# A smaller descriptor ring, five values buffers, tiles at one remainder of 512 bytes, four buffers of activated values, and a copy taken ahead on ScalarE

## The chip, the cores and the metric

The kernel runs on one core of a Trainium2 chip. The metric is the device time of one execution in microseconds. Before the change it is 827.01 us, the median of three runs (826.94 to 827.95).

## What is computed

```
def reference(**kwargs):
    ...
    attn_out = _attn_ref(**attn_kwargs)          # windows of 32 queries, 64 keys each, softmax, times v
    B, H, S, D = attn_out.shape                  # 2, 8, 768, 64
    x = np.ascontiguousarray(attn_out.transpose(0, 2, 1, 3)).reshape(B * S, H * D)
    x = _moe_ref(x=x, **moe_kwargs)              # sum over 4 experts e: p_e * (relu(x @ w1[e]) @ w2[e]), F = 1024
    return _moe2_ref(x=x, **moe2_kwargs)         # h = x @ w_in; (max(h,0) + alpha*min(h,0)) @ w_out, F = 2048
```

1536 tokens of width 512 go through a windowed attention, then through a layer of four weighted experts, then through a second layer with a leaky activation.

## The kernel before

Tokens are the moving side. The two feed-forward layers are cut into 24 slices `p` of the hidden width (16 of the experts, `NP1`, and 8 of the second layer) and each slice into two tiles of 384 columns. One tile is a `gemm1` (seven products of six matmuls, 42 in all, that make four hidden blocks by a scheme with sums of blocks) and a `gemm2` (48 matmuls into `y`, which VectorE adds to `acc`). Every number is split into a high and a low part, `wh`/`wl` for weights, `xh`/`xl` for tokens, `gh`/`gl` in `gg` for hidden values. ScalarE rounds the high part, and GpSimd (at times VectorE) takes the difference. The order of a tile on TensorE is `a b d a c d c`, then `y`.

Attention fills the first 70 us. It is done in twelve units of two halves. SyncE loads queries and keys (`qk`, ring of four halves, `load_half`) and values (`v`, `load_v`); TensorE makes scores (`two`), transposes (`t`), products with the values (`x`) and transposes back (`xt`); five idle matmuls (`keep`) fill each unit's wait. From the ninth unit on, the first expert's tile is mixed in.

Nothing is scheduled by hand in a table: `product` adds an estimated time to `now` for each matmul and, before each, polls streams of other work that are due by then (`prep_poll` for weights and transition, `lag_poll` for the activation steps put off with `later`). What comes out is a fixed program order on each engine, and each engine works it off in order. All transfers are issued from SyncE, one after the other, each on the eighth earlier one's semaphore.

Names that matter below:

- `v_t`: before, halves 0, 1 and 2 of each four stand in buffers of tags `w2`, `w2` and `fr`, the fourth in `w2`; from half 16 (`V_HOME`) in a tile `v4` of tag `S`, set to zero by VectorE when it is made. A values tile is 4160 bytes a partition, so a `w2` or `fr` buffer is 4160 bytes too, though the weights in it take 4096.
- `gelu`: in the second layer ScalarE takes `relu(-h)` out of PSUM (`ACTIVATE g<-a`), multiplies by `-alpha` (`ACTIVATE g<-g,nalpha`), VectorE adds `max(h, 0)`, ScalarE rounds into `gg` and GpSimd takes the rest. `g` has two buffers.
- `act.copy(u2, q["a"])`: the copy of a tile's first product. The second product on bank `a` writes the same bank, so TensorE waits for this copy.
- `prep_w1` for the second slice does not start before the last attention unit has passed its third stage (`att["stage"][NU - 1] > 3`), because it needs the `S` buffer that `v4` holds.

Where the tiles stand in the built program, as the byte address in a partition less the next lower multiple of 512: `xh` and `xl` 0, the ring of first weights 384, the four `w2` buffers 0, 64, 128 and 192, `fr` 256, `ft` 320, `raw` 320 and 384, `gg` of even tiles 0 and of odd tiles 384. In the slices 15 and 17 (`WIDE`) three of the seven first weights stand in `ft` and `fr` buffers instead of the ring (`w` in the rows, not `wh`/`wl`). After the change every one of these is 0.

Of the kernel before, what the change touches and what calls it, by code (L numbers as in the profile page):

```python
# [10 lines left out]
F32 = mybir.dt.float32  # L11
# [3 lines left out]
AF = mybir.ActivationFunctionType  # L15
# [3 lines left out]
B, H, S, D = 2, 8, 768, 64  # L19
# [3 lines left out]
NW = BLK // WIN  # L23
# [5 lines left out]
NU = B * NBLK  # L29
NT, DM = B * S, H * D  # L30
E, F1, F2 = 4, 1024, 2048
P = 128
KD = DM // P
HH = H // 2
HP = HH // 2
QW, KW = HP * BLK, HP * SPAN
NCOL = NT // 2
NP1 = E * F1 // (2 * P)
# [27 lines left out]
def tile_kernel(ctx: ExitStack, tc: tile.TileContext, qk, v, wa, wq, dpt, alpha, out):  # L66
    nc = tc.nc
    scale = 1.0 / float(D) ** 0.5
    pe_, dve, act, pool, sync = (Pinned(tc, e) for e in (nc.tensor, nc.vector, nc.scalar, nc.gpsimd, nc.sync))
# [3 lines left out]
    bp = ctx.enter_context(tc.tile_pool(name="bp", bufs=1))  # L73
# [29 lines left out]
    now = [0.0]  # L103
# [88 lines left out]
    def mm(*a, n, took=None, **kw):  # L192
# [2 lines left out]


    qk_t = [bp.tile([P, QW + KW], F32, tag="ggB", bufs=4, name=f"qk{i}") for i in range(RING)]
    v_t = [bp.tile([P, 2, HP, NW, D + 1], F32, name=f"v{i}", **tag) for i, tag in (
        (3, dict(tag="w2", bufs=4)), (0, dict(tag="w2", bufs=4)), (1, dict(tag="w2", bufs=4)), (2, dict(tag="fr")))]
    v_t = v_t[1:] + v_t[:1]  # L200
    for vt in v_t:
        for e in range(2):
            (pool, dve)[e].memset(vt[:, e], 0.0)
# [3 lines left out]
    pe = pe.rearrange("p (z k e) -> p z k e", e=2, k=KEYS)  # L207

    def v_of(hu):
        return v_t[hu % 4 if hu < V_HOME or hu % 4 < 3 else 4]  # L210

    def load_half(hu):
        if hu >= 2 * NU:
# [5 lines left out]
    def load_v(hu):  # L219
        assert hu == v_next[0]  # L220
        v_next[0] += 1
        if hu >= 2 * NU:
            return
        if hu == V_HOME:
            v_t.append(bp.tile([P, 2, HP, NW, D + 1], F32, tag="S", name="v4"))
            dve.memset(v_t[4], 0.0)
        for e in range(2):
            sync.dma_start(v_of(hu)[e::2, e].rearrange("p z w d -> p (z w d)"), v[hu // 2, e, :, hu % 2])

    def unit(u):  # L230
# [36 lines left out]
        for z in range(2 * HP):  # L267
            half, i = divmod(z, HP)
            if z in CUT:
                n = CUT[z]  # L270
                parts.append((z, n, bank(f"x{u}_{z}")[:, :2 * n * (D + 1)].rearrange("p (z e d) -> p z e d", e=2, d=D + 1)))
            z0, _, x_ps = parts[-1]
            for w in range(NW):
                mm(x_ps[win[w], z - z0], pt[:, z, win[w]], v_of(2 * u + half)[:, :, i, w], n=2 * (D + 1), took=T_X,
                   start=True, stop=True)
            if i == HP - 1:
                load_v(2 * u + half + 4)
        dn = cp.tile([P, 2 * HP, 2, 1], F32, tag="dn", bufs=2, name=f"dn{u}")
        for z, n, x_ps in parts:
            dve.tensor_scalar_add(dn[:, z:z + n], x_ps[:, :, :, D:D + 1], 1e-9)  # L280
# [176 lines left out]
    def pause(t, cond=None):  # L457
        return now[0] + t, cond

    def prep_w1(p):  # L460

        e, dt = pace(p in QUICK, p)
        combine = e
        if p == 1:
            combine = dve
        elif p == NP1:
            combine, dt = dve, DT_NEAR
        if p == NP1 + 2:
            yield pause(0.0, lambda: (NP1, 0) in used1)
        yield pause(0.0, lambda: (p, 0) in raws and (p == 0 or began and landed[p, 0] <= now[0] and att["stage"][NU - 1] > 3))  # L470
        raw = raws[p, 0]
        a11, a12, a22, a21 = (raw[:, i] for i in range(4))
        s = bp.tile([P, 4, 256], F32, tag="S", name=f"s_{p}")
        src = {A11: a11, A12: a12, A22: a22, S1: s[:, 0], S2: s[:, 1], S3: s[:, 2], S4: s[:, 3]}
        for zo, x, y, op in (
            (S1, a21, a22, ALU.add), (S2, s[:, 0], a11, ALU.subtract),
            (S3, a11, a21, ALU.subtract), (S4, a12, s[:, 1], ALU.subtract),
        ):
            combine.tensor_tensor(out=src[zo], in0=x, in1=y, op=op)
            if p:  # L480
                yield pause(dt)
        if p == 0:
            yield pause(4.5)
        for j, z in enumerate(USE):
            yield pause(0.0, lambda: room_w1(p, j))
            h, l = place_w1(p, j)
            act.copy(h, src[z])
            if p:
                yield pause(dt)
            e.tensor_tensor(out=l, in0=src[z], in1=h.bitcast(F32), op=ALU.subtract)  # L490
            w1[p, z] = (h, l)
            yield pause(dt)
        raws.pop((p, 0))
        if p == NP1 + 1:
            load_raw(p, 1)
        elif 0 < p < NP - 1:
            yield pause(0.0, lambda: conv_done(p + 1))
            load_raw(p + 1, 0)
# [131 lines left out]

    glist = []
    lag = []

    def later(t, f):
        lag.append((now[0] + t, f))
        lag.sort(key=lambda x: x[0])

    def lag_poll(until=None):
        while lag and (lag[0][0] <= now[0] or until is not None and not until()):
            lag.pop(0)[1]()  # L640

    def product(*a, n, **kw):
# [6 lines left out]
    def gemm1(p, c0, n, parity, last):  # L649
        cs = slice(c0, c0 + n)  # L650
        nm = f"{p}_{c0}"
        q = {}

        def prod(z, a, b, start, stop):
            if start:
                q[z] = bank(f"{z}{nm}")[:, :n]
            prep_force("w", lambda: (p, a) in w1)
            while p == 0 and b >= T4 and att["x"] < -(-(c0 + n) // BLK):
                att_poll(force=True)
            wh, wl = w1[p, a]  # L660
            k = 0
            for kd in range(2):
                f = slice(kd * P, (kd + 1) * P)
                for w_, x_ in ((wh, xh), (wh, xl), (wl, xh)):
                    product(q[z], w_[:, f], x_[:, 2 * b + kd, cs], n=n,
                            start=start and k == 0, stop=stop and k == 5, skip_group_check=True)
                    k += 1
            if last:
                used1.add((p, USE.index(a)))

        def add(z, other, out):
            dve.tensor_tensor(out=out, in0=q[z], in1=other, op=ALU.add)

        def tmp(name):
            return bp.tile([P, 384], F32, tag=name, name=f"{name}{nm}")[:, :n]

        gs = {}

        def gelu(blk, src):

            i, ab = divmod(blk, 2)

            lag_poll(lambda: len(glist) < 2 or glist[-2][1] in glist[-2][0])
            glist.append((gs, blk))
            if p >= NP1 and i == 0:
                if ab == 0:
                    g2 = bp.tile([P, 2, 384], F32, tag="pb", bufs=2, name=f"g2_{nm}")
                    gs["g2"] = g2
                g = gs["g2"][:, ab, :n]
            else:  # L690
                g = bp.tile([P, 384], F32, tag="g", bufs=2, name=f"g{blk}_{nm}")[:, :n]
            gg = bp.tile([P, 2, 384], F32R, tag="gg" + "AB"[parity], bufs=4, name=f"gg{blk}_{nm}")
            gh, gl = gg[:, 0, :n], gg[:, 1, :n]

            def high():
                act.copy(gh, g)
                pool.tensor_tensor(out=gl, in0=g, in1=gh.bitcast(F32), op=ALU.subtract)
                gs[blk] = (gh, gl)

            def whole():  # L700
                dve.scalar_tensor_tensor(out=g, in0=src, scalar=0.0, in1=g,
                                         op0=ALU.max, op1=ALU.add)
                later(0.8, high)

            if p < NP1:
                pb = pb_t[2 * p * P // F1, c0, n]
                dve.scalar_tensor_tensor(out=g, in0=src, scalar=0.0, in1=pb[:, ab, :n],
                                         op0=ALU.max, op1=ALU.mult)
                later(0.7, high)
            else:  # L710
                fi = 2 * (p - NP1) + i

                act.activation(g, src, AF.Relu, scale=-1.0)
                act.mul(g, g, nalpha[:, fi:fi + 1])
                later(1.4, whole)

        prod("a", A11, B11, True, False)
        u2 = tmp("u2")
        act.copy(u2, q["a"])
        prod("b", S2, T2, True, True)  # L720
        add("b", u2, u2)
        prod("d", S1, T1, True, False)
        t = tmp("t")
        add("d", u2, t)
        prod("a", A12, B21, False, True)
        gelu(0, q["a"])
        prod("c", S3, T3, True, False)
        add("c", t, q["b"])
        prod("d", S4, B22, False, True)
        gelu(3, q["b"])  # L730
        add("d", u2, q["d"])
        prod("c", A22, T4, False, True)
        gelu(1, q["d"])
        add("c", u2, q["c"])
        gelu(2, q["c"])
        return gs
# [120 lines left out]

    for hu in range(RING):
        load_half(hu)
    for hu in range(4):  # L860
        load_v(hu)
    stream("w", weights())
    streams["w"][0] = PREP0
# [79 lines left out]
X_WAIT = (0.0, 7.5)  # L943
DT_NEAR = 0.8
RING = 4
V_HOME = 16
WARM = 18
PAD = 16

# [73 lines left out]
```

## Time and profile before

| | |
|---|---|
| median of three runs | 827.01 us |
| the profiled execution | 827.0 us, span 825.2 us |
| TensorE busy | 812.6 us (98%), 5637 matmuls |
| VectorE, GpSimd, ScalarE busy | 578.7 (70%), 563.5 (68%), 330.8 us (40%) |
| transfers | 71.69 MB, 87 GB/s over the span, but 250 to 280 GB/s in the first 60 us |

A row of the profile is one instruction or a merged run of them. A matmul of 384 columns is listed with 0.34 us, but the next one starts some 0.175 us later, so what a stretch costs TensorE is read from starts, not from durations.

### The profile page before, as it was taken

To read this page: it belongs to the slowest core of one execution; us is meant where nothing else is said; L and a number is where in the kernel's file an instruction comes from. 1 tells how busy PE (TensorE), PEld (TensorE's weight loads), DVE (VectorE), ACT (ScalarE), POOL (GpSimd) and SP (SyncE) were. 2 spreads that over 40 slices of the span, in tenths; PEclk is the share of its full clock that TensorE was granted. 3 is DMA by queue.
4 is the path that set the end of the run, shared out by engine and by line. 5 is a ranking of instruction groups with operands and counts; after the bars stand their busy time and mean duration, and the time that the engine had idled before them with its cause. 6 is when DMAs were issued, how large, how long until landed. Compare 5 with 4: busy or idle time off the path is not lost.

```text
span 825.2 us, 14876 instructions
## 1 busy us (share of the span) xinstructions
PE 812.6 (98%) x5637; PEld 797.0 (97%) x5637; DVE 578.7 (70%) x1116; ACT 330.8 (40%) x718; POOL 563.5 (68%) x586
## 2 busy tenths in 40 slices
PE   8899999999999999999999999999999999999998
PEld 6678999999999999999999999999999999999998
DVE  4687477777777768767777677578954877756555
ACT  3666433223224123232332223145572665455441
POOL 2767777777877877967877872193954987866611
PEclk9999999999999999999999999999999999999999
DMA  7882121331331431322432312001002142211004
GB/s 251 248 279 81 51 90 52 122 115 46 115 103 39 134 116 45 115 71 74 126 102 81 112 37 69 10 26 52 27 26 90 46 122 81 73 40 52 0 1 153
DMA packets 30503, 71.69 MB, mean 87 GB/s; under 512 B 4704, under 2 KB 9952, under 8 KB 30432
## 3 DMA queue, kind: packets, MB, share of 16 engines
q1 hardware_dynamic: 30432, 70.75, 26.5%
q8 instruction: 44, 0.72, 0.4%
q14 instruction: 27, 0.22, 0.1%
HBM read 59.18 MB, written 11.56 MB: 86 GB/s over the span
## 4 chain that ended last, share of the span: by engine, by line
PE 90%; DMA 2%; POOL 2%; ACT 2%; DVE 2%; issue 1%; SPq 1%; ACTq 0%; DVEq 0%; POOLq 0%
PE y L60 47%; PE a L60 12%; PE c L60 11%; PE d L60 11%; PE b L60 6%; POOL gg L60 1%; DMA raw<-in_wa 1%; PE two L60 1%; ACT g L60 1%; DMA qk<-in_qk 1%; PE x L60 1%; DMA v<-in_v 1%; PE t L60 1%; SPq L60 0%; PE wps0.0_84 L60 0%
## 5 line engine op out<-in xcount | busy, mean ns | idle before, releaser
L60 PE MATMUL y<-gg,wh 128*128 128x384 f32 x1540 | 401.1, 337 | 0.7 <-POOL gg L60 0.5
L60 POOL TENSOR_TENSOR gg<-g,gg 128x384 fp32r<-128x384 f32 x192 | 200.9, 1056 | 122.4 <-ACT gg L60 107.8
L60 PEld LDWEIGHTS y<-gg,wh 128*128 128x128 f32 x1540 | 278.8, 188 | 1.8 <-POOL gg L60 1.2
L60 PE MATMUL y<-gg,wl 128*128 128x384 f32 (+1 forms) x770 | 258.6, 336 | 0.0
L60 DVE TENSOR_TENSOR acc<-y,acc 128x384 f32<-128x384 f32 x321 | 171.0, 550 | 53.5 <-PE y L60 52.1
L60 ACT CAST gg<-g 128x384 fp32r<-128x384 f32 x192 | 97.6, 512 | 169.3 <-DVE g L60 169.1
L60 POOL TENSOR_TENSOR wl<-raw,wh 128x256 fp32r<-128x256 f32 (+1 forms) x112 | 114.8, 1034 | 51.4 <-ACT wh L60 37.2
L60 PEld LDWEIGHTS y<-gg,wl 128*128 128x128 f32 x770 | 144.5, 188 | 0.0
L60 ACT COPY u<-a 128x384 f32<-128x384 f32 x48 | 23.0, 479 | 185.4 <-PE a L60 185.4
L60 POOL TENSOR_TENSOR wl<-s,wh 128x256 fp32r<-128x256 f32 x88 | 68.4, 784 | 8.7 <-ACT wh L60 8.1
L60 DVE TENSOR_TENSOR u<-b,u 128x384 f32<-128x384 f32 x48 | 26.7, 557 | 60.6 <-PE b L60 58.1
L60 PE MATMUL a<-xh,wh 128*128 128x384 f32 x184 | 62.4, 339 | 0.4 <-ACT u L60 0.4
L60 PE MATMUL d<-xh,wl 128*128 128x384 f32 x184 | 62.3, 338 | 0.0
L60 PE MATMUL d<-xl,wh 128*128 128x384 f32 x184 | 62.2, 338 | 0.0
L60 PE MATMUL d<-xh,wh 128*128 128x384 f32 x184 | 62.2, 338 | 0.0
L60 PE MATMUL a<-xl,wh 128*128 128x384 f32 x184 | 62.1, 338 | 0.0
L60 PE MATMUL a<-xh,wl 128*128 128x384 f32 x184 | 62.1, 338 | 0.0
L60 ACT CAST wh<-raw 128x256 fp32r<-128x256 f32 (+1 forms) x116 | 54.5, 491 | 15.6 <-PE y L60 14.2
L60 PE MATMUL c<-xh,wh 128*128 128x384 f32 x176 | 59.9, 340 | 0.2 <-DVE b L60 0.2
L60 PE MATMUL c<-xl,wh 128*128 128x384 f32 x176 | 59.5, 338 | 0.0
L60 PE MATMUL c<-xh,wl 128*128 128x384 f32 x176 | 59.5, 338 | 0.0
L60 POOL TENSOR_TENSOR fl<-fl,fm 128x512 f32<-128x512 f32 x32 | 41.4, 1294 | 26.5 <-DVE fm L60 17.5
(117 smaller groups left out, 1363.7 us busy)
## 6 DMA issues: line engine op xcount, KB each, us to landing
fr<-in_wq SPq DMA_DIRECT2D x32, 512.0 KB, 3.9
raw<-in_wa SPq DMA_DIRECT2D x28, 512.0 KB, 3.9
w2s<-fl SPq DMA_DIRECT2D x32, 256.0 KB, 2.4
raw<-w2s SPq DMA_DIRECT2D x16, 512.0 KB, 3.6
qk<-in_qk SPq DMA_DIRECT2D x24, 312.0 KB, 4.6
v<-in_v SPq DMA_DIRECT2D x48, 130.0 KB, 4.1
outT<-acc SPq DMA_DIRECT2D x15, 192.0 KB, 1.8
pb<-p_dram SPq DMA_DIRECT2D x6, 384.0 KB, 3.4
```

The costliest lines, as they stand in the source:

```text
L60: return self.tc.keep_in_program_order(f(*a, **kw))
```

## The change

- The ring that is kept at address 0 of each partition for descriptors of transfers issued by GpSimd is 2048 bytes instead of 16384. No transfer here is issued by GpSimd. 14 KB a partition come free.
- Values get five buffers all through (`RING_V`), two of them of a tag of their own; `v4`, its zeroing in the middle of the attention and `V_HOME` go. `load_v` runs five halves ahead.
- A values tile takes 1152 numbers, 4608 bytes, nine times 512 (`V_ROOM`), so the buffers that it shares with `w2` and `fr` begin at multiples of 512.
- `prep_w1` of the second slice no longer waits for the last unit's third stage.
- `g` has four buffers.
- In the second layer the negative part goes through `later`, and `hold` keeps put-off steps back until a tile's `u2` copy is issued, if nothing forces them.

```diff
+VW = 2 * HP * NW * (D + 1)
...
-    v_t = [bp.tile([P, 2, HP, NW, D + 1], F32, name=f"v{i}", **tag) for i, tag in (
-        (3, dict(tag="w2", bufs=4)), (0, dict(tag="w2", bufs=4)), (1, dict(tag="w2", bufs=4)), (2, dict(tag="fr")))]
-    v_t = v_t[1:] + v_t[:1]
+    v_t = [bp.tile([P, V_ROOM], F32, name=f"v{i}", **tag)[:, :VW].rearrange("p (e z w d) -> p e z w d", e=2, z=HP, w=NW)
+           for i, tag in enumerate((dict(tag="w2", bufs=4), dict(tag="w2", bufs=4), dict(tag="fr"), *2 * [dict(tag="v", bufs=2)]))]
...
-        return v_t[hu % 4 if hu < V_HOME or hu % 4 < 3 else 4]
+        return v_t[hu % RING_V]
...
-        if hu == V_HOME:
-            v_t.append(bp.tile([P, 2, HP, NW, D + 1], F32, tag="S", name="v4"))
-            dve.memset(v_t[4], 0.0)
...
-                load_v(2 * u + half + 4)
+                load_v(2 * u + half + RING_V)
...
-        yield pause(0.0, lambda: (p, 0) in raws and (p == 0 or began and landed[p, 0] <= now[0] and att["stage"][NU - 1] > 3))
+        yield pause(0.0, lambda: (p, 0) in raws and (p == 0 or began and landed[p, 0] <= now[0]))
...
+    hold = [False]
...
-        while lag and (lag[0][0] <= now[0] or until is not None and not until()):
+        while lag and (not hold[0] and lag[0][0] <= now[0] or until is not None and not until()):
...
-                g = bp.tile([P, 384], F32, tag="g", bufs=2, name=f"g{blk}_{nm}")[:, :n]
+                g = bp.tile([P, 384], F32, tag="g", bufs=4, name=f"g{blk}_{nm}")[:, :n]
...
-                act.activation(g, src, AF.Relu, scale=-1.0)
-                act.mul(g, g, nalpha[:, fi:fi + 1])
-                later(1.4, whole)
+                def negative():
+                    act.activation(g, src, AF.Relu, scale=-1.0)
+                    act.mul(g, g, nalpha[:, fi:fi + 1])
+                    later(1.4, whole)
+
+                later(0.0, negative)
+
+        hold[0] = p >= NP1
         prod("a", A11, B11, True, False)
         u2 = tmp("u2")
         act.copy(u2, q["a"])
+        hold[0] = False
...
-    for hu in range(4):
+    for hu in range(RING_V):
         load_v(hu)
...
-V_HOME = 16
+V_ROOM = 1152
+RING_V = 5
...
-    nc = _bacc.Bacc("TRN2", target_bir_lowering=False, num_devices=1)
+    nc = _bacc.Bacc("TRN2", target_bir_lowering=False, num_devices=1, dynamic_dma_scratch_size=2048)
```

TensorE's order does not change anywhere. On SyncE, at the start of the program, these are the issues of before (a `qk` row is one half's queries and keys, two `v` transfers are one half's values, `raw` are weights):

```order
L60 DMA qk3_112<-in_qk 128x624
L60 DMA v0_114<-in_v 64x520 x2
L60 DMA v1_115<-in_v 64x520 x2
L60 DMA v2_116<-in_v 64x520 x2
L60 DMA v3_113<-in_v 64x520 x2
L60 DMA qk0_109<-in_qk 128x624
L60 DMA qk1_110<-in_qk 128x624
L60 DMA raw0_0_179<-in_wa 128x256 x2
```

And now, at the same place:

```order
L61 DMA qk3_112<-in_qk 128x624
L61 DMA v0_113<-in_v 64x520 x2
L61 DMA v1_114<-in_v 64x520 x2
L61 DMA v2_115<-in_v 64x520 x2
L61 DMA v3_116<-in_v 64x520 x2
L61 DMA v4_117<-in_v 64x520 x2
L61 DMA qk0_109<-in_qk 128x624
L61 DMA qk1_110<-in_qk 128x624
L61 DMA raw0_0_184<-in_wa 128x256 x2
```

The fifth half's two transfers stand ahead of the third unit's `qk`, and all later `qk` and `raw` transfers of the attention stand two places further back.

On ScalarE, at the border of the two tiles of slice 18 in the second layer (`a18_384` is the next tile's first product, `c18_0` this tile's last), before:

```order
L60 ACTIVATE g2_18_0_7470<-g2_18_0_7470,nalpha_83 128x384
L60 CAST gg3_18_0_7495<-g3_18_0_7494 128x384
L60 ACTIVATE g2_18_0_7520<-c18_0_7474 128x384
L60 ACTIVATE g2_18_0_7520<-g2_18_0_7520,nalpha_83 128x384
L60 COPY u218_384_7533<-a18_384_7524 128x384
L60 CAST gg1_18_0_7513<-g2_18_0_7470 128x384
```

And now:

```order
L61 ACTIVATE g2_18_0_7471<-g2_18_0_7471,nalpha_83 128x384
L61 CAST gg3_18_0_7496<-g3_18_0_7495 128x384
L61 COPY u218_384_7532<-a18_384_7523 128x384
L61 ACTIVATE g2_18_0_7521<-c18_0_7473 128x384
L61 ACTIVATE g2_18_0_7521<-g2_18_0_7521,nalpha_83 128x384
L61 CAST gg1_18_0_7514<-g2_18_0_7471 128x384
```

The copy passes the two steps of the last block. The same happens at two more borders, from tile 16 to 17, first and second half; elsewhere ScalarE's order in the second layer stays, since a `gemm2` lies between the tiles.

## Rows read from the trace of the kernel before

**Rows 1.** The page, part 4: shares of the span in the chain that ended last.
```profile
PE 90%; DMA 2%; POOL 2%; ACT 2%; DVE 2%; issue 1%; SPq 1%; ACTq 0%; DVEq 0%; POOLq 0%
```

**Rows 2.** Stretches: length, busy us (instructions) by engine, PE clock, DMA share, GB/s.
```profile
33.00:40.00 7.00, 4.79 (x86) 4.05 (x87) 2.37 (x8) 2.71 (x7) 3.94 (x4) 0.76 0.86 222
40.00:60.00 20.00, 18.06 (x418) 15.30 (x402) 16.27 (x42) 12.49 (x25) 14.13 (x13) 1.00 0.89 284
80.00:540.00 460.00, 459.83 (x2622) 459.22 (x2621) 332.58 (x626) 141.45 (x315) 333.23 (x343) 1.00 0.25 82
560.00:592.00 32.00, 30.79 (x172) 29.77 (x171) 28.60 (x52) 20.90 (x46) 19.37 (x16) 1.00 0.15 50
```

**Rows 3.** Chain of waits, 660 to 810 us: start us, us, engine, tile, count.
```profile
671.55 1.06 PE a L60 x6
...
678.95 8.36 PE y L60 x48
...
694.69 8.42 PE y L60 x48
...
710.51 8.43 PE y L60 x48
...
726.33 8.36 PE y L60 x48
...
797.79 1.06 PE a L60 x6
```

**Rows 4.** Timeline of PE at matmuls whose operands stand elsewhere: start, us, instruction.
```profile
7.14 0.86 PE L60 MATMUL keep<-xh 128*128 128x384 f32 x4
...
5.97 2.03 PE L60 MATMUL keep<-xh 128*128 128x384 f32 x10
...
516.32 0.34 PE L60 MATMUL c<-xh,w 128*128 128x384 f32 x1
...
517.36 0.34 PE L60 MATMUL y<-gg,wh 128*128 128x384 f32 x1
...
545.16 0.34 PE L60 MATMUL a<-xl,w 128*128 128x384 f32 x1
...
547.94 0.34 PE L60 MATMUL d<-xh,w 128*128 128x384 f32 x1
...
613.77 0.35 PE L60 MATMUL c<-xh,w 128*128 128x384 f32 x1
...
614.84 0.34 PE L60 MATMUL y<-gg,wh 128*128 128x384 f32 x1
```

**Rows 5.** Chain of waits in the attention: start us, us, what.
```profile
8.80 5.68 DMA qk<-in_qk
...
29.61 5.50 DMA v<-in_v
...
46.05 4.82 DMA raw<-in_wa
...
50.90 0.62 ACT wh L60
```

**Rows 6.** Timeline of SyncE's queue, the first values' issues.
```profile
3.06 5.01 SPq L60 DMA_DIRECT2D v<-in_v  x8
```

**Rows 7.** Timeline of VectorE, the zeroing of the late values buffer.
```profile
42.89 0.93 DVE L60 MEMSET v<- 128x1040 f32 x1 [0.17 <-issue]
```

**Rows 8.** Timelines of PE and VectorE where TensorE waits late: in brackets idle before, releaser.
```profile
543.34 0.56 DVE L60 SCALAR_TENSOR_TENSOR g<-c,pb 128x384 f32<-128x384 f32 x1 [0.52 <-POOL gg L60]
...
577.45 0.45 PE L60 MATMUL a<-xh,w 128*128 128x384 f32 x1 [0.42 <-ACT u L60]
...
581.27 0.44 PE L60 MATMUL c<-xh,w 128*128 128x384 f32 x1 [0.43 <-DVE b L60]
...
589.11 0.62 PE L60 MATMUL y<-gg,wh 128*128 128x384 f32 x2 [0.36 <-POOL gg L60]
...
642.80 0.45 PE L60 MATMUL a<-xh,wh 128*128 128x384 f32 x1 [0.44 <-ACT u L60]
```

## The prediction

> **What bounds the kernel now.** I read the chain of waits first: 90% of the span is TensorE, and no other engine has more than 2% [rows 1]. Next the table by stretches: from 80 to 540 us TensorE is idle for 0.17 of 460 us; it loses 2.2 us between 33 and 40, 1.9 between 40 and 60 and 1.2 between 560 and 592 [rows 2]. So there are three things to win: the few waits, the attention's start, and the distance from one matmul to the next in the 90% where nothing waits. The last is the largest. The change leaves TensorE's order and its matmuls as they are, so this distance is all that it can alter there.
>
> From tile to tile the chain repeats: eight tiles take 797.79 - 671.55 = 126.24 us, 15.78 a tile, or 175.3 ns for each of its 90 matmuls [rows 3]. Inside this regular stretch the `y` blocks are not equal: 8.36, 8.42, 8.43, 8.36 us for 48 matmuls [rows 3]. The work is the same; what differs is where the operands stand. In the slow two one weight buffer has the same remainder of 512 as `gg`, or lies 256 from it (weights 192 and 0 with `gg` at 0; 64 and 128 with `gg` at 384); in these fast two none has (192 and 0 with 384; 64 and 128 with 0). So the remainder of weights against moving tokens sets the distance, by up to 1.5 ns (0.07 us over 48).
>
> **Part 1: all large tiles at remainder 0.** `gemm1` now reads weights at 384 against tokens at 0; after the change both are at 0, in `gemm2` too. No tile of before has that for all its weights, so I bound it by the nearest rows.
> - The floor: with weights at 320 and tokens at 0, sixteen steps take 547.94 - 545.16 = 2.78 us, 173.75 ns each [rows 4]. With weights at 256 and tokens at 0, six steps from 516.32 to 517.36 take 1.04 us, 173.3 ns [rows 4].
> - The ceiling: the same pair of buffers, 613.77 to 614.84, takes 1.07 us, 178.3 ns [rows 4].
> - The only stretch with both operands at 0 is `keep`: ten matmuls take 2.03 us, of which the last four take 0.86 [rows 4]. Less 0.34 for the listed length of the last one, these four have three steps in 0.52 us, 173.3 ns. The six steps ahead of them take 1.17 us, 195 ns each.
>
> The last row decides for me: an equal remainder starts with long steps and then settles at 173.3 to 173.8. The start is paid after a disturbance; the settled distance is paid thousands of times. I take 173.4. A tile then costs 90 x 0.1734 = 15.61 us instead of 15.78, 0.17 less; for 47 tiles (the first lies inside the attention) this is **-8.0 us**. The step's bounds are 173.0 (the shortest of these rows, with their rounding) and 178.3 (a state that never settles), -9.9 and +12.5 us; within the forecast I let it reach 174, -5.6.
>
> A page speaks against this part. The Trainium skill, page "SBUF — State Buffer", section "Who interferes with whom", says that TensorE has two independent read ports, one for the moving operand and one for the weights' load, and that only the port pair shared by VectorE and GpSimd contends. By it the place of an operand changes nothing, this part is worth 0, and the sum ends at 826.1; the `y` blocks, 8.36 against 8.43 us, do not agree with it [rows 3].
>
> **Part 2: values run five halves ahead.** This adds one half's two transfers ahead of the third unit's `qk`; no transfer is added in total, and the zeroing of the late buffer moves to the start, beside the warm-up. SyncE issues eight values transfers in 5.01 us, 0.63 each [rows 6], so two cost it 1.25 us; in bytes they are 0.27 MB, 1.0 us at 284 GB/s [rows 2]. The early `qk` transfer is already in the chain at 8.80 [rows 5], so the third unit's scores come up to 1.25 us later. What is late next is the value transfer that ends at 35.11 (29.61 + 5.50) [rows 5]: TensorE waits for it now and the clock falls to a mean of 0.76 there [rows 2]. It keeps its place in the queue, since the extra half ahead of it is itself one that was due before it, so a later start is absorbed by that wait.
>
> The zeroing in the middle (0.93 us on VectorE at 42.89) goes [rows 7]; it stands ahead of a unit's normalising and delays TensorE by somewhat less. This gain I count at nothing, because the chain then runs through the transfer of the first slice's second weights, 46.05 to 50.87, and the ScalarE cast on it at 50.90 [rows 5]. Queued behind that cast in ScalarE's order is the copy of the ninth unit's transposed scores, for which TensorE waits. The `raw` transfer stands two transfers further back after the change, so it lands 0 to 1.25 us later; with SyncE issuing and the transfers flowing all the time (DMA share 0.89 [rows 2]) I take **+0.9 us**, near the price in bytes, bounds 0 and +1.25 us. Everything won before 50.9 is hidden by this, the lost clock too.
>
> **Part 3: four `g` buffers, and the copy first.** The late waits of TensorE cost more than the idle time in brackets. A matmul is listed with 0.34 us but the next starts 0.17 after it, and the first after a wait takes 0.11 longer (0.45 [rows 8]), so an idle of 0.42 loses 0.42 + 0.17 + 0.11 = 0.70 us.
> - 642.80: `a` waits for the copy `u` behind two steps of the last block, 0.44 idle, 0.72 lost [rows 8]. The copy now passes both: -0.7.
> - 577.45: the same, 0.70 lost [rows 8]. Here I count nothing: `c` at 581.27 waits for VectorE (0.43 idle) [rows 8], whose work is queued behind a difference on a ScalarE cast that the swap doesn't bring forward. The wait moves there.
> - 589.11: `y` waits for GpSimd's `gg`, 0.36 idle, 0.64 lost [rows 8]. the swap brings a cast of tokens, and so GpSimd's difference of them, ahead of the last block, and GpSimd's queue is done sooner: -0.6.
> - `g`: VectorE at 543.34 waited 0.52 us for GpSimd to give back a buffer [rows 8], with the copy for the next tile and a sum queued behind; four buffers end this wait: -0.5.
>
> Sum **-1.8 us**; bounds 0 (each wait replaced) and -3.2 (all won, 577.45 and 581.27 too).
>
> **Part 4: the rest at nothing.** The smaller ring is not used by any transfer. The earlier start of the second slice's weights only moves VectorE and ScalarE work to a time when TensorE has a full tile ahead of it; without that cover it would cost one VectorE step, half a microsecond.
>
> **The sum,** against the profiled execution's 827.0 us (its span is 825.2; the median of the runs is 827.01, so nothing has to be converted): 827.0 - 8.0 + 0.9 - 1.8 = 818.1. I forecast **818 us**; by its bounds most of this case lies between 815 and 822.
>
> **The rivals.**
> - *The remainder is worth nothing.* Steps stay at 175.3 ns: 827.0 + 0.9 - 1.8 = 826.1. For it: most fast `y` rows differ by only 0.07 us in 8.4. Against it: the same rows repeat tile after tile. Chance 0.14.
> - *Equal remainders are the slow case,* and the kernel gets slower: TensorE's loads of weights and tokens meet, as in the slow `y` blocks, 8.43 us, which have just one weight buffer equal, and in 613.77. At 175.9 ns (midway between 173.4 and 178.3) a tile takes 15.83 us, +0.05, times 47 is +2.4; with the other terms 828.5. At 178.3 ns a tile takes 16.05, and the sum is 838.6. It decides from 175.5 ns up, where +0.9 us eats what parts 2 and 3 leave. Chance 0.16; for it speaks that every row with a partly equal pair is slow, against it that `keep` ends fast.
> - *The fifth buffer does what its name says:* the values wait at 35 and the fallen clock go (2.2 us idle plus the slow stretch), and the `raw` transfer isn't later. Then part 2 is 0 instead of +0.9, 817. This stays inside the forecast's bounds; more is capped by the transfer that lands at 50.87.
> - *The attention loses more* (clock falls a second time, each `qk` late): +3 instead of +0.9, 820; inside the bounds too.
>
> **How the numbers follow.** Forecast (settled steps of 173 to 174 ns) 0.66, no effect of the remainder 0.14, equal is slow 0.16, other 0.04. A measurement of this kernel tells 0.2%, 1.65 us, from no change. Faster by more: the forecast and two fifths of the second case, 0.72. Within 0.2%: the rest of the second case and a fourth of the third, 0.13. Slower by more: 0.15. The range reaches from 815 to 826.5: below it lie the ends of the forecast's bounds, above it the slow case, together about 2 in 10.
>
> **What would show it.** In the chain of the changed kernel a tile between 660 and 800 us takes 15.6 us and all `y` blocks last the same, about 8.32; 15.8 would show the second case, 15.85 or more and equal `y` blocks the third. ScalarE's cast of the second weights at 50.9 comes up to 1.25 us later. The waits at 577 and 642 for `u` are gone, the one on VectorE near 581 is longer, and VectorE has no long MEMSET after the start. Wrong would be the whole forecast if the settled end of `keep` is owed to its own tiles (zeros, one moving tile) and not to the remainder.

## The result, and the profile after

The changed kernel takes 818.73 us, the median of four runs (817.69 to 820.61), against 826.98 us for the kernel before on the same chip (825.76 to 827.95). The ratio is 0.9904, with a 95% interval of 0.988 to 0.9927. The profiled execution took 819.24 us, its span is 817.4 us instead of 825.2.

The chain of waits between 660 and 812 us, columns as in [rows 3]:

```profile
703.94 8.32 PE y L61 x48
712.26 1.04 PE a L61 x6
...
719.54 8.32 PE y L61 x48
727.86 1.04 PE a L61 x6
...
735.14 8.32 PE y L61 x48
...
750.74 8.32 PE y L61 x48
```

All `y` blocks last the same, 8.32 us, where they were 8.36 to 8.43, and six matmuls of a product take 1.04 us, where they took 1.06 [rows 3]. A tile takes 750.74 - 735.14 = 15.60 us, or 173.3 ns a matmul.

The stretches of [rows 2] in the changed kernel, with the same columns:

```profile
33.00:40.00 7.00, 6.86 (x213) 5.61 (x212) 5.48 (x14) 6.03 (x13) 6.35 (x9) 1.00 0.77 197
40.00:60.00 20.00, 16.28 (x356) 13.80 (x355) 14.92 (x39) 10.69 (x21) 13.67 (x12) 1.00 0.91 293
80.00:540.00 460.00, 459.79 (x2652) 459.17 (x2651) 340.19 (x635) 144.82 (x323) 337.54 (x348) 1.00 0.26 82
560.00:592.00 32.00, 30.42 (x174) 29.78 (x173) 26.46 (x44) 20.08 (x41) 23.06 (x20) 1.00 0.14 50
```

Between 33 and 40 us TensorE no longer waits and its clock stays at 1.00. Between 40 and 60 it now loses 3.7 us instead of 1.9: what was won is given back. Between 560 and 592 it is idle for 1.6 us, where it was 1.2.

The balance: the first `y` block of the first tile starts at 64.08 us in the kernel before and at 64.41 now, so the attention is 0.3 us longer. From there to the start of the last matmul it was 757.88 us (to 821.96) and is 749.77 (to 814.18), 8.1 us less. In this part the late waits are worth as much as before. I add up, after 450 us, what every step from one matmul to the next takes above 0.176 us, where it is at least 0.03 more, and call this the lost time: 3.69 us before, 3.71 now. (One wait ahead of that, at 433 to 437 us, hangs on a transfer and is missing in three of the profiles, so it is left out.) So the whole gain is the shorter step.

### The profile page after: what moved, and what is told of

Its sections match the earlier page's. It is cut to its first block, busy times and chain, and to the rows that moved or that the text cites. A ratio compares the mean times of both kernels' runs of the same rounds, so it can differ in the third digit from the quotient of the medians.

```text
span 817.4 us, 14838 instructions
## 1 busy us (share of the span) xinstructions
PE 801.4 (98%) x5637; PEld 787.0 (96%) x5637; DVE 584.5 (72%) x1116; ACT 330.8 (40%) x718; POOL 563.5 (69%) x587
## 4 chain that ended last, share of the span: by engine, by line
PE 88%; DVE 3%; POOL 3%; ACT 2%; DMA 2%; issue 1%; SPq 0%; DVEq 0%; POOLq 0%; ACTq 0%
PE y L61 47%; PE a L61 11%; PE c L61 11%; PE d L61 11%; PE b L61 6%; DMA raw<-in_wa 2%; POOL gg L61 1%; DMA qk<-in_qk 1%; POOL s L61 1%; PE two L61 1%; PE x L61 1%; DVE pe L61 1%; DVE mx L61 0%; PE wps0.0_84 L61 0%; POOL wl L61 0%
```

## The experiments

All edits but the first two start from the changed kernel.

### The distance by remainder, measured alone

The computation is left out; only matmuls from one large tile of ones are issued:

```diff
+    def group(name, wr, xr, pool_):
+        q = pool_.tile([P, N], F32, tag="ps", name=name)
+        for k in range(48):
+            w = big[:, 4096 + wr // 4 + (k % 6) * 128:][:, :128]
+            x = big[:, xr // 4 + (k % 2) * 512:][:, :N]
+            pe_.matmul(q, w, x, start=k % 6 == 0, stop=k % 6 == 5, skip_group_check=True)
+        act.copy(sink, q)
```

> This kernel leaves out all of the computation and times matmuls alone: 48 matmuls of 384 columns in 32-bit numbers for each remainder of the weights from 0 to 480 in steps of 32 bytes, with the moving tokens at remainder 0 (groups a), with the tokens at 128 (groups b), and once more with the tokens at 0 and a wait ahead of each group (groups c). Theory, the distance from one matmul to the next is set by the weights' remainder less the tokens': a0 and a256 settle at 173.3 ns, a320 at 173.8, a384 at 176 (the rows of the kernel before), and b at 128 more repeats a (b128 as a0). Rival, the place is of no matter: all groups agree within 0.1 ns. The prediction also says that an equal remainder starts with long steps after a wait: c0 would then be longer than a0 by more than the others are, some 0.1 us.

Mean distance of the 47 steps of each group, from the starts in the trace, in ns. For the groups c the first step, the one after the wait, is left out; it takes 0.28 us at every remainder. The first group c follows no wait.

```
weights at        0    32    64    96   128   160   192   224
a, tokens 0   173.3 173.3 174.6 176.6 176.1 176.7 173.2 176.6
c, tokens 0   173.4 173.4 174.6 173.3 175.5 176.7 173.3 176.7
b, tokens 128 175.9 176.7 173.3 176.6 173.8 173.3 174.6 176.6
weights at      256   288   320   352   384   416   448   480
a, tokens 0   173.8 173.3 174.6 176.6 176.1 176.6 173.2 176.6
```

The chain shows whole groups c; these are the weights at 32, 64, 96, 128 and 160, each with its wait ahead (start, us, what):

```profile
297.83 8.61 PE c L28 x48
...
307.06 8.66 PE c L28 x48
...
316.33 8.60 PE c L28 x48
...
325.54 8.70 PE c L28 x48
...
334.85 8.76 PE c L28 x48
```

The rival falls. The pattern repeats after 256 bytes, not 512, and moving the tokens by 128 moves it by 128: what counts is the weights' address less the tokens', modulo 256. The differences 0, 32 and 192 are fast, 128, 160 and 224 slow (175.5 to 176.7 ns), by up to 3.4 ns. At 96 there are two distances, 176.6 in the run of groups and 173.3 after a wait, so there the way in which a row of matmuls starts decides too. The kernel before read its first weights at 384 against tokens at 0, a difference of 128: 42 x 176.1 ns = 7.40 us, and its tile less its `y` block, 15.78 - 8.39, is 7.39.

The table is of groups in which every step has the same difference, and it does not give the `y` blocks of the kernel before, in which two weight buffers alternate. By the addresses in the prediction the slow two (8.42 and 8.43 us, [rows 3]) have the differences 192 and 0, both 173.3 in the table, and the fast two (8.36) have 64 and 128, 174.6 and 176.1. The table would make the first pair 8.32 and the second 8.40 to 8.43. So what is left as the cause there is that the difference changes from step to step, which no run here measures alone. Per tile the `y` blocks hold 0.07 us of the gain (8.39 to 8.32) and the products the other 0.11, which the table explains.

The expected long start at an equal remainder is there, but small. Group a at 0 begins with steps of 173 and 174 ns; it follows a group at the same difference, and the first group c follows no wait. The test is weights at 256. After a group at another remainder (group a) the first three steps take 185, 175 and 182 ns, some 20 ns in all; after a wait (group c) the first six take 278, 178, 185, 176, 181 and 174. The changed kernel has the same after its wait at 576.42 us: 282, 178, 185, 175, 182, 173. Expected was some 0.1 us more than at other remainders; it is 0.02 to 0.03.

### The alignment alone

The kernel before, with the small ring and padded values tiles; four values buffers, the late zeroing, two `g` buffers and the old order on ScalarE stay:

```diff
-    v_t = [bp.tile([P, 2, HP, NW, D + 1], F32, name=f"v{i}", **tag) for i, tag in (
+    v_t = [bp.tile([P, 1152], F32, name=f"v{i}", **tag)[:, :2 * HP * NW * (D + 1)].rearrange("p (e z w d) -> p e z w d", e=2, z=HP, w=NW) for i, tag in (
...
-            v_t.append(bp.tile([P, 2, HP, NW, D + 1], F32, tag="S", name="v4"))
+            v_t.append(bp.tile([P, 1152], F32, tag="S", name="v4")[:, :2 * HP * NW * (D + 1)].rearrange("p (e z w d) -> p e z w d", e=2, z=HP, w=NW))
...
-    nc = _bacc.Bacc("TRN2", target_bir_lowering=False, num_devices=1)
+    nc = _bacc.Bacc("TRN2", target_bir_lowering=False, num_devices=1, dynamic_dma_scratch_size=2048)
```

> The kernel before with the small descriptor ring and values tiles of 1152 numbers, so that every large tile stands at remainder 0; four values buffers, the late zeroing, two g buffers and the old order on ScalarE stay. Theory, the step carries the gain: y blocks 8.32 us, tiles 15.60, 47 x 0.17 = 8 us less, 819.0 (818.0 to 820.0), with the waits of before at 33, 577, 589 and 642 us (shifted by what is gained). Rival, the gain comes from the values buffers or from ScalarE's order: 826 to 827.

Measured: 818.50 us (818.46 to 820.70), ratio 0.9907 (0.9882 to 0.9931): the whole gain, with nothing of the other parts. Its timeline of TensorE has the late waits of [rows 8] again; the two for `u` are a little longer, those for `b` and `gg` a little shorter or the same:

```profile
571.01 0.45 PE L60 MATMUL a<-xh,w 128*128 128x384 f32 x1 [0.46 <-ACT u L60]
...
574.82 0.44 PE L60 MATMUL c<-xh,w 128*128 128x384 f32 x1 [0.40 <-DVE b L60]
...
582.95 0.61 PE L60 MATMUL y<-gg,wh 128*128 128x384 f32 x2 [0.36 <-POOL gg L60]
...
636.15 0.45 PE L60 MATMUL a<-xh,wh 128*128 128x384 f32 x1 [0.49 <-ACT u L60]
```

The lost time is 4.22 us instead of 3.69: a TensorE that is faster waits longer for engines that are not. The wait for values at 33 us did not come back as expected; in its place are three of 0.28, 0.71 and 0.47 us (at 33.20, 37.97 and 43.51).

### The change without the padding

```diff
-V_ROOM = 1152
+V_ROOM = 1040
```

> The changed kernel with values tiles of 1040 numbers: the w2 buffers stand at 0, 64, 128 and 192, the first weights and the odd tiles' gg at 448, tokens and even gg at 0. All else of the change stays. Theory: y blocks between 8.34 and 8.43 us again, the products between 1.04 and 1.06 us for six, the time between 821 and 826. Rival, the remainder is worth nothing: 818.7 as the changed kernel.

Measured: 823.50 us (822.32 to 826.42). The chain of waits:

```profile
690.77 8.43 PE y L61 x48
699.20 1.04 PE a L61 x6
...
706.48 8.41 PE y L61 x48
```

The `y` blocks are slow again. The products stay at 1.04: weights at 448 against tokens at 0 are a difference of 192 modulo 256, fast in the sweep too. From the first `y` block to the last matmul it is 752.88 us against 749.77, so 3.1 of the 8.1 us are gone with the padding alone (more by the medians, which hold the attention too): neither the ring nor the buffers carry them.

### All tiles moved by 64 bytes

```diff
-PAD = 16
+PAD = 32
```

> The changed kernel with 64 bytes more in front of all large tiles, so that every one stands at remainder 64. Theory, only the difference of weights and tokens counts: y blocks 8.32 us, 15.60 a tile, 818.7 as the changed kernel (within 1.0). Rival, tiles must begin at a multiple of 512 themselves: y blocks 8.36 or more, 820 to 827.

```profile
690.41 8.32 PE y L61 x48
698.73 1.04 PE a L61 x6
...
706.01 8.32 PE y L61 x48
```

The steps are those of the changed kernel, so tiles need not begin at a multiple of 512. The median is 821.44 us (819.24 to 823.43), above the 818.7 that I expected: in this profile the first `y` block comes at 66.44 us and the clock is 0.86 between 40 and 64 us. From that block to the last matmul it is 749.81 us, as in the changed kernel (749.77). So the excess is the attention's, which the next runs are about.

### Four values buffers instead of five

```diff
-           for i, tag in enumerate((dict(tag="w2", bufs=4), dict(tag="w2", bufs=4), dict(tag="fr"), *2 * [dict(tag="v", bufs=2)]))]
+           for i, tag in enumerate((dict(tag="w2", bufs=4), dict(tag="w2", bufs=4), dict(tag="fr"), dict(tag="v", bufs=1)))]
...
-RING_V = 5
+RING_V = 4
```

> The changed kernel with four values buffers instead of five (two w2, fr, one of a tag of its own) and values loaded four halves ahead; alignment and part 3 stay. Theory, the fifth buffer costs what its two extra transfers ahead of the qk transfers take: the attention ends 0.9 to 1.6 us earlier than in the changed kernel (first y block of the first tile at 62.8 to 63.5 us instead of 64.4), 817.5 (816.7 to 818.3). Rival, the fifth buffer pays: TensorE waits for values again at 33 to 38 us, 819 to 820.

Measured: 817.38 us (816.35 to 817.91), ratio 0.9879 (0.9865 to 0.9894), the lowest median of all the kernels. The chain of waits with four buffers:

```profile
33.05 2.60 issue
35.65 0.66 PE x L61 x12
...
50.69 0.79 PE two L61 x53
51.48 0.55 PE d L61 x2
52.03 1.02 PE x L61 x32
```

And that of the changed kernel:

```profile
43.59 1.14 PE x L61 x32
...
45.73 4.78 DMA raw<-in_wa
...
50.54 0.62 ACT wh L61
...
52.00 1.09 PE x L61 x32
```

With four buffers TensorE stands still for 2.60 us at 33.05; with five it does not, and its seventh unit's `x` comes at 38.23 instead of 40.52. But the ninth unit's `x` comes at 52.03 with four and at 52.00 with five, since the changed kernel then waits for the second weights and the cast on them. With four buffers these weights are issued at 43.99 instead of 45.73 us, and the cast on them doesn't wait:

```profile
49.87 0.61 ACT L61 CAST wh<-raw 128x512 fp32r<-128x512 f32 x1
```

So two different chains end at 52.0 by chance: with five buffers the one through the weights, with four TensorE's own, which holds the stop at 33.05. This stop is not the wait for values that the rival expected. It has no releaser on record, it comes after 20 of the sixth unit's 32 matmuls of `x`, four of them in its second half, and the values of this unit's second half had landed by 31.98. The two runs of part 3 below, with five buffers, have such a stop in `x` too (2.60 and 2.20 us). A true wait for values is in the profile of the last run below, with four buffers:

```profile
34.65 0.96 PE L61 MATMUL x<-v,pt 128*32 128x130 f32 x16 [2.20 <-DMA v<-in_v]
```

The first `y` block comes at 63.60 us with four buffers and at 64.41 with five. Most of this 0.8 arises late: the twelfth unit's scores start at 60.43 and 60.51, and the next product 0.79 and 1.51 us after that, since TensorE stops within the scores of the changed kernel (last section).

### The changed kernel again

> The changed kernel once more, on the same chip as the next run, to tell how far its attention varies from execution to execution: if the first y block comes again at 64.4 us the fifth buffer's cost is steady and the time 818.7 (817.7 to 819.7); if it comes anywhere from 62.9 to 65.3, as over the kernels run so far, one profile of the attention can't price an edit of it.

Measured: 820.39 us (818.18 to 823.99), ratio 0.9917 (0.9897 to 0.9938). In this profile the first `y` block comes at 68.08 us, later than either case had it and 3.7 later than in the other profile of the same kernel. Its chain of waits, and stretches of 4 us with the columns of [rows 2]:

```profile
47.19 6.05 DMA raw<-in_wa
...
53.26 0.62 ACT wh L61
...
54.72 1.96 PE x L61 x32
```

```profile
48.00:52.00 4.00, 1.52 (x67) 0.89 (x66) 2.19 (x5) 0.00 (x0) 0.00 (x0) 0.95 0.86 279
52.00:56.00 4.00, 1.28 (x24) 1.18 (x28) 0.00 (x0) 2.74 (x6) 1.74 (x2) 0.50 0.81 243
56.00:60.00 4.00, 4.00 (x33) 3.48 (x22) 2.30 (x7) 0.95 (x3) 3.94 (x4) 0.69 0.98 317
```

Here the second weights start 1.46 us later and land 2.73 later than in the other profile. TensorE is busy for 1.52 and 1.28 us of two stretches of four, and the granted clock falls to 0.50, its lower level of 1.2 GHz; 32 matmuls of `x` then take 1.96 us instead of 1.09.

Over all profiles the first `y` block starts with four values buffers at 62.83, 62.88, 63.58, 63.60 and 64.08 us; with five at 63.47 (the run with the late fifth half, below), 63.96, 64.36, 64.39, 64.41, 65.30, 66.44 and 68.08. One profile doesn't price an edit of the attention; these thirteen put the fifth buffer's cost at about 0.8 us in the median (64.40 against 63.58), and two of the eight lie 2.9 and 4.5 above the median with four. The times agree: with all tiles aligned, the medians are 817.38 to 818.50 us with four buffers (four kernels) and 818.73 to 821.44 with five (818.74 for the one single execution), though some of these kernels differ in more than the buffers.

### The fifth half issued later

```diff
-    for hu in range(RING_V):
+    for hu in range(RING_V - 1):
         load_v(hu)
...
         *[(x, lambda: load_raw(0, 0, 4)) for x in (1, 1)],
+        (1, lambda: load_v(RING_V - 1)),
```

> The changed kernel with five values buffers, but the fifth half's two transfers issued after the third unit's qk and the first half of the first raw weights, instead of ahead of them. Theory, the fifth buffer costs because its two transfers stand ahead of what the early units need: the third unit's scores come at 12.9 to 13.2 us instead of 13.8, the first raw weights no later than with four buffers, the first y block at 62.9 to 63.6 us, 817.5 (816.5 to 818.5). Rival, five halves ahead push back every later qk and raw transfer wherever the extra half is issued: the ninth unit's x still at 52 us or later, 818.7 to 820.4, with executions as far apart as those of the changed kernel.

Measured: 819.18 us (818.39 to 819.96). The third unit's scores come at 12.91 us as expected, and the lateness comes elsewhere: the fifth unit's at 22.62 and the sixth's at 29.67, against 21.59 and 27.22 with four buffers. The median is the rival's. But the profiled execution is the fastest of the six, and its first `y` block, 63.47 us, lies where the theory had it, with the ninth unit's `x` at 51.68. So the run doesn't decide whether the fifth half has to be paid for wherever it is issued.

### The second weights issued one unit earlier

```diff
-        *[(x, lambda: load_raw(0, 1, 2)) for x in (8, 8)],
...
+        *[(x, lambda: load_raw(0, 1, 2)) for x in (7, 7)],
         *[(x, lambda ab=ab: load_pb(0, *FIRST[0], (ab,))) for ab, x in enumerate((7, 7))],
```

> The changed kernel with the two transfers of the first slice's second weights issued one unit earlier, ahead of the expert weights' broadcast (pb) of the first tile and of two qk and two v transfers. Theory of the prediction, all that is won before 51 us is hidden behind that transfer, because the ninth unit's x waits for the ScalarE cast on it: the cast comes 1.5 to 3 us earlier, x of the ninth unit at 52.0 about 1 us earlier, and the total is 817.7 (817.0 to 818.3). Rival, what is moved behind it (pb, qk, v) is late instead: 818.7 or more.

Measured: 819.25 us (817.66 to 820.17), in the rival's range, though 0.5 us from the changed kernel is not clear of the spread. The weights no longer stand in the chain, `qk` does:

```profile
45.33 5.54 DMA qk<-in_qk
...
52.82 3.67 DMA qk<-in_qk
```

The ninth unit's `x` comes 0.15 us earlier, at 51.85, and the first `y` block 0.9 later, at 65.30; half of this is a longer stop within the last unit's scores (0.93 us idle instead of 0.49). In this profile `qk` is late where the weights were: putting one transfer ahead put another behind.

### Part 3 undone, and its halves

```diff
-                g = bp.tile([P, 384], F32, tag="g", bufs=4, name=f"g{blk}_{nm}")[:, :n]
+                g = bp.tile([P, 384], F32, tag="g", bufs=2, name=f"g{blk}_{nm}")[:, :n]
...
-                later(0.0, negative)
+                negative()
...
-        hold[0] = p >= NP1
...
-        hold[0] = False
```

> The changed kernel with two g buffers and the old order on ScalarE; alignment and five values buffers stay. By the trace of the changed kernel against that with the alignment alone: the waits for u at 571 and 636 us come back and those for c shrink, the stalls after 75 us sum to 4.9 us instead of 4.2, +0.7: 819.4 (818.7 to 820.1). Rival, the prediction's step: +1.8, 820.5. Rival, part 3 is worth nothing: 818.7, the same sum of stalls.

Measured: 820.58 us (819.27 to 822.42), span 817.9 in the profile. The four waits stand as in the run with the alignment alone, and the lost time is 3.95 us; in the changed kernel it is 3.71, and its second profile, the early weights' and that with 64 bytes more agree (3.70 to 3.75). In the changed kernel, timelines of TensorE around 543, 576, 584 and 640 us:

```profile
543.52 0.44 PE L61 MATMUL c<-xh,w 128*128 128x384 f32 x1 [0.32 <-DVE b L61]
...
576.42 0.45 PE L61 MATMUL c<-xh,w 128*128 128x384 f32 x1 [1.43 <-DVE b L61]
...
583.98 0.62 PE L61 MATMUL y<-gg,wh 128*128 128x384 f32 x2 [0.15 <-POOL gg L61]
...
640.14 0.45 PE L61 MATMUL c<-xh,wh 128*128 128x384 f32 x1 [0.29 <-DVE b L61]
```

Both waits for `u` are gone, and `c` waits in their place: 1.43 us idle at 576.42, 0.29 at 640.14. VectorE's timeline there:

```profile
574.50 1.39 DVE L61 TENSOR_TENSOR xl<-st,xh 128x512 fp32r<-128x512 f32 x1 [1.08 <-ACT xh L61]
575.81 0.55 DVE L61 TENSOR_TENSOR b<-c,t 128x384 f32<-128x384 f32 x1
```

The sum `b` stands behind a difference `xl` that waits 1.08 us for ScalarE's cast. From these sums part 3 is worth 0.2 us (3.95) to 0.5 (4.22 with the alignment alone). The whole stretch from the first `y` block to the last matmul says 0.55 (750.32 against 749.77) and 0.75 (750.52). The medians differ by 1.9 us, the number of the rival that is the prediction's step, but they hold the spread of the attention too; in the two profiles the attention ends alike (64.36 and 64.41).

The same with only the `g` buffers put back to two:

```diff
-                g = bp.tile([P, 384], F32, tag="g", bufs=4, name=f"g{blk}_{nm}")[:, :n]
+                g = bp.tile([P, 384], F32, tag="g", bufs=2, name=f"g{blk}_{nm}")[:, :n]
```

> The changed kernel with two g buffers; the copy first on ScalarE stays. Theory, what part 3 wins is won by the copy alone: the waits for u stay away, and the stalls of TensorE after 400 us sum to the 4.1 us of the changed kernel within 0.2. Prediction: 0.5 us more, since VectorE waits at 543 us for a g buffer and c behind it.

One execution took 818.74 us; the lost time is 3.96 us, and the waits for `u` at 577 and 642 stay away. At 543 us the loss only changes its place: 0.31 us at `a` (539.51) and 0.31 at `c` (542.95) with two buffers, 0.58 at `c` with four. Of the 0.25 us more, 0.15 is a step at 464 us that only the run with the late fifth half has too, so four `g` buffers are worth some 0.1.

### Two tries at the wait of c

Both with four values buffers. First the steps of the transition's first half further apart, then those of the second half:

```diff
-DT_X = (1.1, 0.88)
+DT_X = (1.3, 0.88)
```

> Four values buffers as in the run with them, and the steps of the transition into the second layer 1.3 instead of 1.1 us apart, which moves VectorE's difference of tokens (xl) behind the sum b for which TensorE waits at 576 us. Theory: the waits of TensorE at 543 and 576 us (0.6 and 1.7 us lost) shrink to 0.5 together, 1.5 us less than with four values buffers alone, 816.0 (815.3 to 817). Rival: the wait moves on to u or y, 817.5 as with four values buffers alone.

```diff
-DT_X = (1.1, 0.88)
+DT_X = (1.1, 1.05)
```

> Four values buffers, and the transition's steps for the second half of the columns 1.05 instead of 0.88 us apart, which puts VectorE's sum b ahead of the difference xl (and ScalarE's cast for it behind two steps of the activation). Theory: c at 576 us waits because b stands behind xl, which waits 1.08 us for that cast and then takes 1.39; with b ahead the 1.70 us lost there fall to 0.3, and 816.0 (815.3 to 816.8) is left. Rival: c waits for ScalarE's or GpSimd's queue whichever way VectorE is ordered, 817.4 as with four values buffers alone.

Measured: 818.27 (817.72 to 818.64) and 818.24 us (818.04 to 819.11). Neither is faster than four buffers alone, so both theories fail. The first leaves the wait of `c` as it is (1.43 us idle at 575.88; it hangs on the steps of the second half) and brings a wait of `a` for `u` at 539.60, 0.59 us idle; the lost time is 4.18 us. The second ends that wait, and TensorE's timeline has these instead:

```profile
580.72 0.61 PE L61 MATMUL y<-gg,wh 128*128 128x384 f32 x2 [0.48 <-POOL gg L61]
582.13 0.62 PE L61 MATMUL y<-gg,wh 128*128 128x384 f32 x2 [0.62 <-POOL gg L61]
...
594.60 0.44 PE L61 MATMUL b<-xl,wh 128*128 128x384 f32 x1 [0.38 <-DVE xl L61]
```

The lost time is 4.00 us, against 3.71 with four buffers alone. In both tries the delay came out at another matmul (`a`, then `y` and `b`) instead of going away, as the rivals had it.

## Why the prediction was right, step by step

- **Part 1, -8.0 us: right.** The tile is 15.60 us against 15.61, the step 173.3 ns against 173.4, and the gain from the first `y` block on is 8.1 us. The alignment alone gives it, moving all tiles together keeps it, taking the padding away loses 3.1 us of it. The row that decided was read too narrowly: I took the settled end of `keep` as the evidence and named the weights at 256 (173.3 ns, [rows 4]) only as a floor. The sweep shows that 256 and 0 are the same case, so that row had been the measurement itself. The ceiling, 178.3 ns in [rows 4], is six steps right after a change of remainder, 185, 176, 182, 173, 173 and 176 ns in the trace. The sweep shows the same three long steps (185, 175 and 182), never a state that stays. The 195 ns at the start of `keep` are the mean of 279, 177, 185, 176, 182 and 173, which is the sweep's start after a wait at 256, step by step: one first step that every remainder has, and the same three. So the start costs 0.13 us once, and the choice of the settled end was sound. One reading did not hold: that in the `y` blocks an equal remainder, or one 256 away, makes the slow pair. Measured alone, these differences are the fastest; that their alternation makes the pair slow is what remains, not shown by a run of its own.
- **The rivals on the remainder fall.** The first, after the Trainium skill, page "SBUF — State Buffer", section "Who interferes with whom", needed steps that don't depend on the operands' place. The sweep's trace disagrees, 173.3 against 176.6 ns. The second, an equal remainder as the slow case, has an equal pair at 173.3.
- **Part 2, +0.9 us: the size is right, the way only sometimes.** The profile has +0.3 against the one profile of before, and all profiles together some 0.8. I said that the early delay is absorbed and that the second weights land later. In the first profile they land 0.4 us earlier (50.51 against 50.87, [rows 5]); in the second 2.4 us later (53.24), with the clock's fall that I had as the last rival. That what is won before is hidden behind these weights holds for the changed kernel: its seventh unit's `x` comes 2.0 us earlier than before (38.23 against 40.26), its ninth only 0.36 (52.00 against 52.36), with the cast on the weights in the chain. With four buffers the weights are earlier and a stop of TensorE takes their place, so the equal 52.0 there is no proof. Much of the cost that the profiles show, 0.7 of the 0.8 us between the changed kernel and the one with four buffers, is a stop within the last unit's scores, which no term of mine held. So the third rival, the fifth buffer that pays, had its mechanism and not its gain.
- **Part 3, -1.8 us: wrong in size.** It is -0.2 to -0.5 by the lost time, -0.55 to -0.75 by the whole stretch. The step that failed is the sum of four waits as if each were a loss of its own. I had moved the wait at 577 to `c`, and it moved there, but grew from 0.43 to 1.43 us idle, because `b` had a step ahead of it on VectorE that waits for ScalarE. At 642.80 (0.72 lost) nothing seemed late next; 0.27 us at `d` and 0.56 at `c` came in its place. At 589 the loss fell from 0.62 to 0.43. The `g` buffers gave 0.1 instead of 0.5. And the shorter step made the waits longer by about as much as part 3 takes away (3.69 us of lost time before, 4.22 and 3.95 with the step and without part 3), which no term of mine held: an engine that is sped up takes the cover from the others.
- **The sum** held because part 1, by far the largest term, was right. In this profile it is 827.0 - 8.1 + 0.3 = 819.2: the late waits as a whole gave nothing where I had -1.8, and the attention cost 0.6 less than I had. That the two misses offset each other in part is luck. In the second profile of the same kernel, 822.4 us, the attention cost 4.0.

## What to carry to other kernels

Where TensorE never waits, look at the distance from start to start: at equal work it differed by 2% with the addresses of weights and tokens modulo 256, and giving all of them one remainder by padding a shared buffer set it right. Waits behind engines that are nearly as busy can't be added up as gains; follow each to what is late next on the same chain, and expect them to grow when the waiting engine gets faster. A prefetch that runs further ahead takes its place in a full transfer queue from something else; price it there, and from several profiles. And two chains that end at the same time are not one cause: look at what each waits for before calling a wait free.

## What had not been expected of the hardware

- In groups of one difference the distance between matmuls of 384 columns in 32-bit numbers follows the weights' address less the tokens', modulo 256 bytes: 173.3 ns at 0, 32 and 192, 174.6 at 64, 175.5 to 176.7 at 128, 160 and 224, and at 96 either 173.3 or 176.6, by how the row began. Blocks that alternate between two differences don't take the mean: 175.5 ns for the two slow `y` blocks of before, with 192 and 0.
- The first step after a wait takes 0.28 us instead of 0.17 at every remainder; at a difference of 0 some 0.02 us more follow in the next steps.
- In three profiles, the changed kernel, the run with the earlier weights and that with two `g` buffers, TensorE stops for 0.49, 0.93 and 0.43 us within one unit's scores with no releaser on record, each time after the same 21 matmuls. The first, in the chain of waits of the changed kernel:

```profile
60.58 0.34 PE two L61 x21
60.92 0.49 issue
61.41 0.69 PE two L61 x41
```

The traces point to what such stops wait for. The profile also lists transfers in a queue that it names `instruction`; in the changed kernel the window from 59.0 to 60.2 us has this row for it (transfers, MB, share):

```profile
q8 instruction: 1, 0.02, 5.0%
```

This one of 16 KB ends at 60.06, and TensorE goes on at 61.41, 1.35 us later. In the attention the thirteen traces have 24 stops of TensorE of 0.15 us or more without a releaser, the 2.60 us with four values buffers among them, and each ends 1.26 to 1.56 us after the end of such a 16 KB transfer. These transfers come several us apart. That fits TensorE waiting for instructions that come late while data fill the transfer engines; no run here shows it, since none moves these transfers.
